# Issuing the remainder-row scores of each eight-unit group two units later, directly ahead of the first scores that use the same K

## The chip, the cores and the metric

The kernel runs on one core of a Trainium2 chip. The metric is the device time of one execution in microseconds (us). Before the change, three runs gave 1204.64, 1207.65 and 1207.88 us, with a median of 1207.65 us.

A core has five engines that matter here, each with an instruction queue of its own that runs in order: TensorE (PE; its weight loads are listed apart as PEld), VectorE (DVE), ScalarE (ACT), GpSimd (POOL) and SyncE (SP), which issues most of the DMA transfers. They are tied together by semaphores alone. Matmul results go to PSUM, which this kernel divides into eight banks with fixed uses; everything else on the chip lies in SBUF.

## The reference, cut to what matters

Two attention blocks, A and B, of the same shape are computed, and their outputs are placed side by side. There are 16 batches, 144 query rows per batch, 16 heads of width 256, 512 keys, and a model width of 448; all data are bf16.

```python
q = (x @ wq).reshape(B, Sq, H, Dh).transpose(0, 2, 1, 3)
scores = einsum("bhqd,bhkd->bhqk", q, k_cache) * (Dh ** -0.5)
p = softmax(scores, axis=-1)
o = einsum("bhqk,bhkd->bhqd", p, v_cache)
out = o.transpose(0, 2, 1, 3).reshape(B, Sq, H * Dh) @ wo
# out = concatenate([out_A, out_B], axis=-1)
```

(`_B_ref` repeats K and V by a factor of 1, so B is A with other data.)

## The kernel before, in words

The work is cut into 512 **units**; a unit is one head of one batch of one block (2 x 16 x 16). The units are numbered in the order block, batch, head. The 144 query rows of a unit are more than one 128-partition tile takes comfortably, so they are split into 112 rows (`QA`), handled unit by unit, and 32 remainder rows (`QB`), handled together: the remainder rows of four units fill one 128-partition tile. The code calls four units G and eight units SG (or n); the 64 groups of eight units share one K tile each, which one transposing DMA loads (`t_load_k`, L368). `kt_sb` has room for three such tiles.

The steps of a unit U and the lines where the profile shows them:

- Q (`t_q`, L398): eight matmuls of the projection into the bank `qp_ps`; a scaled copy to `qt_sb` on DVE (L411) or ACT (L415). `qt_sb` holds 12 units.
- SA (`t_sa`, L516): two matmuls, scores of the 112 rows, into one of two banks `sa_ps`, by the parity of U.
- the row maximum on DVE (`t_max`, L528), the exponential with row sum on ACT (`t_exp`, L539), the reciprocal on DVE (L549), the normalisation on POOL (`t_norm`, L557).
- TA (`t_ta`, L570): four transposes of the 112 rows into the other `sa_ps` bank, and a copy to `pt_sb` on DVE (L580).
- PV (`t_pv`, L603): eight matmuls with V into `ot_ps`, and a copy into `ring` on ACT (L618, L620).
- OP (`t_op_piece`, L641): the output projection of finished 128-row chunks, a few matmuls at a time; the result goes out through ACT (L659) and a store issued from POOL (L671).

The remainder rows of a group n of eight units have their own chain:

- SB (`t_sb`, L440): 16 matmuls of 32 columns, four side by side in the array, which write both `sb_ps` banks, one for each four units. It reads the K tile of group n and the remainder rows in `qt_sb` of all eight units.
- for each of the two fours (G = 2n and 2n + 1): the maximum on DVE (`t_max_b`, L453), the exponential on ACT (`t_exp_b`, L463), the reciprocal on DVE (L473), the normalisation on POOL (`t_norm_b`, L481), the transposes TB on PE (`t_tb`, L493), which write the same `sb_ps` bank, and a copy to `pt_sb` on DVE (`t_evac_ptb`, L502).

The order of the instructions is written out by a loop over **slots** i, from -8 up to the end, with one unit in each stage of a software pipeline per slot. In slot i, PE gets Q of unit i + 15, then SB if a group's slot is i, then SA of unit i + 5, TA of unit i + 2, TB if one is due, PV of unit i, and then OP pieces if any are ready. DVE gets, in that order, the reciprocals of the remainder rows, the scaled copy of Q (in slots that are 2, 4, 6 or 7 modulo 8; in the others ACT has it), the maximum, the reciprocal, the copy after TA, the copy after TB and the maximum of the remainder rows. `_Sched` records this order and adds the semaphore waits that the data and the banks need. Three constants name the lags:

```python
LQ, LS, LT = 15, 5, 2
LSB = 7
```

`LS` is the lag of SA. SB of group n stood in slot 8n - `LSB`; the first two groups have slots of their own (-5 and 3). The rest of the chain hangs on that slot:

```python
s0 = sb_slot[n] + 2 * h          # h = 0, 1; G = 2n + h
at(mxb_at, s0, G); at(exb_at, s0 + 1, G); at(nmb_at, s0 + 2, G)
at(tb_at, max(s0 + 3, 8 * n - 4 + 4 * h), G)
```

OP pieces are ready two slots after the last head of a batch, that is from slots that are 1 modulo 16, and are paced by a credit of 2.25 pieces per slot. In the first 128 slots they run out in the 11th slot, so slots that are 11 to 15 and 0 modulo 16 have none; later there are mostly one or a few such slots per batch.

DMA loads are planned with a slot of release and a deadline (`plan`), sorted by deadline, and all issued from SP, which works them off in order and waits on the semaphores of the buffers that they overwrite. The deadline of a K tile is 8n - `LSB`. x tiles (L294, L295) come every 64 units, the weights of block B (L272, L274) around the middle.

Of the kernel before, what the change touches and what calls it, by code (L numbers as in the profile page):

```python
# [122 lines left out]
def bass_concat_heads__mha_block_cached__gqa_block_cached__near_ridge_kernel(  # L123
# [37 lines left out]
    LQ, LS, LT = 15, 5, 2  # L161
    LSB = 7
# [10 lines left out]
    NSG = NT // 8  # L173
# [4 lines left out]
    with contextlib.ExitStack() as es:  # L178
# [503 lines left out]
        def plan(lo, deadline, lead, fn, *args):  # L682
            dma_plan.append((deadline, len(dma_plan), lo, lead, fn, args))

        sb_slot = [8 * n - LSB for n in range(NSG)]
        sb_slot[0:2] = [-LS, 3]
        q_slot = [u - LQ for u in range(NT)]
        q_slot[0:24] = [-7] * 4 + [-6] * 4 + [-5, -5, -4, -4, -1, -1, 0, 0] + [3, 4, 4, 5, 6, 6, 7, 8]
# [233 lines left out]
```

## Time and profile before

| | |
|---|---|
| three runs, median | 1207.65 us (1204.64 to 1207.88) |
| the profiled execution | 1205.52 us, span 1203.8 us |
| PE busy | 1183.8 us, 98% of the span |
| PEld, DVE, ACT, POOL busy | 75%, 64%, 63%, 56% |
| granted TensorE clock | 1.000 |
| chain that ended last | PE 88%, DMA 6%, DVE 3%, SP queue 3% |
| SA matmuls, mean of one | 385 ns, 1024 of them |
| SB matmuls, mean of one | 382 ns, 1024 of them, four at a time |

In rows of the timeline the first number is the start in us from the start of the span, the second the time in us, then engine, line, operation, destination <- sources, shape and count; in square brackets stands idle time of the engine ahead of the row and what ended it. Matmul starts are recorded while their ends are modelled, so distances between starts are the safer reading on PE.

### The profile page before, as it was taken

Reading aid. Unit: us, or ns where it says so; the run is one execution under the profiler, and the core shown is the slowest. Engines: PE = TensorE matmul, PEld = TensorE weight load, DVE = VectorE, ACT = ScalarE, POOL = GpSimd, SP = SyncE. Lnnn points to the kernel's source line nnn. Section 1 sums busy time; section 2 is a strip of 40 time slices with the busy share of each in tenths; the row PEclk is TensorE's granted clock in tenths of the full one; section 3 lists DMA queues with packets and bytes.
Section 4 is the critical chain, followed back from the end, with each engine's and each line's share of the span. In section 5 each row is a group of like instructions: output and inputs, shape, how many; then the busy total and the mean of one; then the engine's idle time right before and its main releaser. Section 6 shows DMA issues by size and latency. Waiting matters only on the chain.

```text
span 1203.8 us, 34217 instructions
## 1 busy us (share of the span) xinstructions
PE 1183.8 (98%) x14116; PEld 901.8 (75%) x14116; DVE 776.3 (64%) x2190; ACT 762.2 (63%) x2222; POOL 678.4 (56%) x680
## 2 busy tenths in 40 slices
PE   7899999999999999999999999999999999999998
PEld 5677777777777777777777777777777777777776
DVE  4666676666666666666566666666666666666664
ACT  4666666666666666666666666666666666666654
POOL 0565565565565565565555655655655655655554
PEclk9999999999999999999999999999999999999999
DMA  9999999999999999899999999999999999999971
GB/s 304 287 270 280 241 250 244 229 234 241 265 226 227 246 259 246 225 240 234 284 299 265 276 264 272 246 233 238 241 256 230 245 228 261 242 227 244 240 187 48
DMA packets 611130, 294.09 MB, mean 244 GB/s; under 512 B 529696, under 2 KB 538720, under 8 KB 610976
## 3 DMA queue, kind: packets, MB, share of 16 engines
q1 hardware_dynamic: 609344, 288.01, 100.6%
q0 software_dynamic: 1632, 3.90, 1.4%
q8 instruction: 112, 1.84, 0.6%
q14 instruction: 42, 0.34, 0.1%
HBM read 153.61 MB, written 4.13 MB: 131 GB/s over the span
## 4 chain that ended last, share of the span: by engine, by line
PE 88%; DMA 6%; DVE 3%; SPq 3%; ACT 0%; issue 0%; POOL 0%; DVEq 0%
PE ot_ps L603 19%; PE sa_ps L516 18%; PE qp_ps L398 18%; PE op_ps L641 17%; PE sa_ps L570 8%; PE sb_ps L440 5%; DMA kt_sb<-in_B_k_cache_dram 3%; DMA kt_sb<-in_A_k_cache_dram 2%; PE sb_ps L493 2%; DVE stat L528 1%; SPq L294 1%; DMA wq_sb<-in_A_wq_dram 1%; SPq L295 1%; PE qp_ps L641 0%; DVE pt_sb L580 0%; SPq L272 0%
## 5 line engine op out<-in xcount | busy, mean ns | idle before, releaser
L557 POOL TENSOR_TENSOR pa_sb<-pa_sb,stat 112x512 bf16<-112x512 bf16 x512 | 532.6, 1040 | 515.2 <-DVE stat L549 488.5
L539 ACT ACTIVATE pa_sb<-sa_ps,stat 112x512 bf16<-112x512 f32 x512 | 352.0, 688 | 407.3 <-DVE stat L528 406.4
L528 DVE TENSOR_REDUCE stat<-sa_ps 112x1 f32<-112x512 f32 x512 | 353.7, 691 | 321.8 <-PE sa_ps L516 318.6
L398 PEld LDWEIGHTS qp_ps<-xt_sb,wq_sb 128*128 128x128 bf16 x4032 | 283.3, 98 | 80.0 <-DMA wq_sb<-in_A_wq_dram 2.6
L603 PE MATMUL ot_ps<-pt_sb,v_sb 128*128 128x144 bf16 x4096 | 340.4, 226 | 0.0
L398 PE MATMUL qp_ps<-xt_sb,wq_sb 128*128 128x144 bf16 x4032 | 334.5, 226 | 5.6 <-DMA wq_sb<-in_A_wq_dram 3.0
L516 PE MATMUL sa_ps<-kt_sb,qt_sb 128*112 128x512 bf16 x1024 | 310.8, 385 | 0.6 <-DVE pt_sb L580 0.2
L641 PE MATMUL op_ps<-wo_sb,ring 128*128 128x448 bf16 x1120 | 278.8, 352 | 0.0
L603 PEld LDWEIGHTS ot_ps<-pt_sb,v_sb 128*128 128x128 bf16 x4096 | 268.5, 97 | 0.4
L570 PEld LDWEIGHTS sa_ps<-ident,pa_sb 112*128 112x128 bf16 x2048 | 145.4, 97 | 111.0 <-ACT pa_sb L539 23.7
L618 ACT ACTIVATE ring<-ot_ps 128x288 bf16<-128x288 f32 (+8 forms) x512 | 190.3, 372 | 4.4 <-PE ot_ps L603 4.4
L580 DVE COPY pt_sb<-sa_ps 128x448 bf16<-128x448 bf16 x512 | 190.3, 372 | 2.4 <-PE sa_ps L570 2.4
L570 PE MATMUL sa_ps<-ident,pa_sb 112*128 112x112 bf16 x2048 | 185.4, 212 | 0.2
L411 DVE TENSOR_SCALAR qt_sb<-qp_ps 128x288 bf16<-128x288 f32 x250 | 114.1, 457 | 79.4 <-PE qp_ps L398 78.5
L481 POOL TENSOR_TENSOR pb_sb<-pb_sb,stat 128x512 bf16<-128x512 bf16 x128 | 133.1, 1040 | 0.1
L516 PEld LDWEIGHTS sa_ps<-kt_sb,qt_sb 128*112 128x112 bf16 x1024 | 97.0, 129 | 38.7 <-issue 27.2
L641 PEld LDWEIGHTS op_ps<-wo_sb,ring 128*128 128x128 bf16 x1120 | 95.1, 98 | 27.6 <-ACT ring L618 0.2
L415 ACT ACTIVATE qt_sb<-qp_ps 128x288 bf16<-128x288 f32 x254 | 105.2, 414 | 15.5 <-PE qp_ps L398 13.3
L539 ACT ACTIVATION_READ_ACCUMULATOR pa_sb<-sa_ps,stat 112x1 f32 x512 | 99.0, 193 | 0.0
L463 ACT ACTIVATE pb_sb<-sb_ps,stat 128x512 bf16<-128x512 f32 x128 | 88.5, 692 | 0.0
L453 DVE TENSOR_REDUCE stat<-sb_ps 128x1 f32<-128x512 f32 x128 | 86.9, 679 | 0.0
L549 DVE RECIPROCAL stat<-stat 112x1 f32<-112x1 f32 x512 | 78.3, 153 | 0.7 <-ACT pa_sb L539 0.7
(49 smaller groups left out, 420.4 us busy)
## 6 DMA issues: line engine op xcount, KB each, us to landing
v_sb<-in_A_v_cache_dram SPq DMA_DIRECT2D x64, 1024.0 KB, 6.0
v_sb<-in_B_v_cache_dram SPq DMA_DIRECT2D x64, 1024.0 KB, 6.0
out_dram<-ost_sb POOLq DMA_DIRECT2D x34, 112.0 KB, 5.4
wo_sb<-in_A_wo_dram SPq DMA_DIRECT2D x8, 448.0 KB, 6.8
wo_sb<-in_B_wo_dram SPq DMA_DIRECT2D x8, 448.0 KB, 6.1
wq_sb<-in_A_wq_dram SPq DMA_DIRECT2D x4, 768.0 KB, 12.1
wq_sb<-in_B_wq_dram SPq DMA_DIRECT2D x4, 768.0 KB, 7.4
kt_sb<-in_A_k_cache_dram SPq DMA_DIRECT2D x2, 1024.0 KB, 11.0
```

The costliest lines, as they stand in the source:

```text
L398: ins = t.matmul(acc[:, dc * SQ:(dc + 1) * SQ], lhsT=wq_sb[:, kc, c0:c0 + 128], rhs=xt_sb[:, xsl, kc, xo:xo + SQ], start=(kc == 0 and dc = ...
L411: return v.tensor_scalar(qt_sb[:, sl, :, :], src, 1.0 / 16.0, None, op0=ALU.mult)
L481: return g.tensor_tensor(pb_sb[:, psl, :], pb_sb[:, psl, :], stat[:, RINVB + sl:RINVB + sl + 1].to_broadcast([128, SK]), op=ALU.mult)
L516: ins = t.matmul(sa_ps[bank][0:QA, :].rearrange("q (k r) -> q k r", k=KR), lhsT=qt_sb[:, U % NQT, dc, 0:QA], rhs=kt_of(U, dc), start=(dc = ...
L528: return v.tensor_reduce(stat[0:QA, NEG + sl:NEG + sl + 1], sa_ps[bank][0:QA, :], axis=AX.X, op=ALU.max, negate=True)
L539: return a.activation(pa_sb[0:QA, psl, :], sa_ps[bank][0:QA, :], AF.Exp, bias=stat[0:QA, NEG + sl:NEG + sl + 1], scale=1.0, accum_out=stat ...
L557: return g.tensor_tensor(pa_sb[0:QA, psl, :], pa_sb[0:QA, psl, :], stat[0:QA, RINV + sl:RINV + sl + 1].to_broadcast([QA, SK]), op=ALU.mult)
L570: ins = t.transpose(pta_ps[bank][:, c * 128:c * 128 + QA], src[:, c, :], ident[0:QA, 0:QA])
L580: return v.tensor_copy(pt_sb[:, sl, :, 0:QA], pta_ps[bank][:, 0:512].rearrange("p (c q) -> p c q", c=4)[:, :, 0:QA])
L603: ins = t.matmul(ot_ps[ob][:, dc * SQ:(dc + 1) * SQ], lhsT=v_sb[:, vsl, j, c * DH + dc * 128:c * DH + (dc + 1) * 128], rhs=pt_sb[:, sl, c, ...
L618: ins = a.activation(ring[:, 2 * h:2 * h + 2, c0:c0 + n1], src[:, :, 0:n1], AF.Copy)
L641: ins = t.matmul(acc[0:m, 0:D], lhsT=ring[:, c, col0:col0 + m], rhs=wo_sb[:, c, :], start=(c == first), stop=(c == last))
```

## The change

SB of group n moves from slot 8n - 7 to slot 8n - 5, the slot in which SA of unit 8n stands; within the slot SB is ahead of SA. Groups 0 and 1 keep their slots, so 62 of the 64 groups move.

```diff
-        sb_slot = [8 * n - LSB for n in range(NSG)]
+        sb_slot = [8 * n - LS for n in range(NSG)]
         sb_slot[0:2] = [-LS, 3]
```

With SB move, by the same two slots, the maximum, exponential, reciprocal and normalisation of both fours. TB of the first four and the copy after it move from slot 8n - 4 to 8n - 2. TB of the second four stays in slot 8n, as the later of the two terms of `max` is now equal to the earlier. Nothing is added or removed, and `LSB` remains in the deadline of the K loads, so SP's list of DMAs is the same, in the same order.

## The prediction

> **What bounds the kernel now.** I read the page first, then the list of waits, then the timeline of PE around each SB. The page says that PE has almost no idle time to give back. The list of waits says what PE and its weight loads still wait for at SB (L440); columns after the colon are us in total, times, longest.
>
> ```profile
> PE 1183.8 (98%) x14116; PEld 901.8 (75%) x14116; DVE 776.3 (64%) x2190; ACT 762.2 (63%) x2222; POOL 678.4 (56%) x680
> ```
>
> ```profile
> PEld sb_ps L440 <- DVE pt_sb L502: 5.0, 16, 0.9
> ...
> PE sb_ps L440 <- DMA kt_sb<-in_B_k_cache_dram: 3.5, 3, 1.7
> ...
> PE sb_ps L440 <- DMA kt_sb<-in_A_k_cache_dram: 1.8, 2, 1.1
> ```
>
> SB is thus the one place in the steady part where PE waits: five times for a K tile, and 16 times (weight loads only) for the copy after the last TB, which frees the bank. What a wait costs I read from starts on PE, as the distance from the Q ahead of SB to SB. The first pair below waits for nothing (0.60 us), the other five for K.
>
> ```profile
> 127.76 0.66 PE L398 MATMUL qp_ps<-xt_sb,wq_sb 128*128 128x144 bf16 x8
> 128.36 1.05 PE L440 MATMUL sb_ps<-kt_sb,qt_sb 128*32 128x512 bf16 x16
> ...
> 288.40 0.66 PE L398 MATMUL qp_ps<-xt_sb,wq_sb 128*128 128x144 bf16 x8
> 289.81 1.05 PE L440 MATMUL sb_ps<-kt_sb,qt_sb 128*32 128x512 bf16 x16 [0.74 <-DMA kt_sb<-in_A_k_cache_dram]
> ...
> 579.38 0.66 PE L398 MATMUL qp_ps<-xt_sb,wq_sb 128*128 128x144 bf16 x8
> 581.15 1.05 PE L440 MATMUL sb_ps<-kt_sb,qt_sb 128*32 128x512 bf16 x16 [1.10 <-DMA kt_sb<-in_A_k_cache_dram]
> ...
> 599.33 0.66 PE L398 MATMUL qp_ps<-xt_sb,wq_sb 128*128 128x144 bf16 x8
> 601.70 1.05 PE L440 MATMUL sb_ps<-kt_sb,qt_sb 128*32 128x512 bf16 x16 [1.70 <-DMA kt_sb<-in_B_k_cache_dram]
> ...
> 618.05 0.66 PE L398 MATMUL qp_ps<-xt_sb,wq_sb 128*128 128x144 bf16 x8
> 619.39 1.05 PE L440 MATMUL sb_ps<-kt_sb,qt_sb 128*32 128x512 bf16 x16 [0.67 <-DMA kt_sb<-in_B_k_cache_dram]
> ...
> 728.96 0.66 PE L398 MATMUL qp_ps<-xt_sb,wq_sb 128*128 128x144 bf16 x8
> 730.81 1.05 PE L440 MATMUL sb_ps<-kt_sb,qt_sb 128*32 128x512 bf16 x16 [1.18 <-DMA kt_sb<-in_B_k_cache_dram]
> ```
>
> The distances are 1.41, 1.77, 2.37, 1.34 and 1.85 us; less 0.60 each they are 0.81, 1.17, 1.77, 0.74 and 1.25, together 5.7 us. Two of the loads as the chain of waits has them:
>
> ```profile
> 277.09 12.59 DMA kt_sb<-in_A_k_cache_dram
> ...
> 601.33 17.92 DMA kt_sb<-in_B_k_cache_dram
> ```
>
> **The change part by part: the K waits.** SB is the first reader of a K tile; SA of unit 8n reads it two slots later. The change lets SB wait where SA needs the tile anyway, and SP's list and its deadlines stay. A load's landing doesn't move, its first reader does. How much later that is, Q starts two slots after three of the stalls show:
>
> ```profile
> 586.83 0.66 PE L398 MATMUL qp_ps<-xt_sb,wq_sb 128*128 128x144 bf16 x8
> ...
> 606.62 0.66 PE L398 MATMUL qp_ps<-xt_sb,wq_sb 128*128 128x144 bf16 x8
> ...
> 625.82 0.66 PE L398 MATMUL qp_ps<-xt_sb,wq_sb 128*128 128x144 bf16 x8
> ```
>
> From 579.38 to 586.83 are 7.45 us; without the stall (1.17) and without SB itself (1.05) 5.2 us. In the same way 606.62 - 599.33 gives 4.5 and 625.82 - 618.05 gives 6.0. These three loads follow one another, so stalls that vanish add up against the next: the second would be late by 1.77 + 1.17 = 2.9 against 4.5 us, the third by 0.74 + 2.9 = 3.7 against 6.0. The two single ones, 0.81 and 1.25, stand against at least two shortest slots of 1.78 us each (below). No K wait is left; the nearest has 1.6 us to spare. Bounds: -5.7 if all go, 0 if all come back behind slower transfers; I take -5.7, as all five have cover. Behind SB nothing new waits: SA of unit 8n is next on PE and needs the same tile.
>
> By the Trainium skill, "DMA: Bandwidth & Descriptors", Latency and other measured facts, a transposing DMA reaches 261 GB/s; a K tile of 2.1 MB would then take an estimated 8.0 us, land at 285.1, and there would be no K wait to remove, a sum of about 1205 us. The row of 12.59 us is 167 GB/s, so I go by the row.
>
> **The copy that frees the bank.** SB in slot 8n - 7 stands one slot behind TB of the second four. In slots without OP pieces that is too near:
>
> ```profile
> 144.17 0.66 PE L398 MATMUL qp_ps<-xt_sb,wq_sb 128*128 128x144 bf16 x8
> 144.88 1.05 PE L440 MATMUL sb_ps<-kt_sb,qt_sb 128*32 128x512 bf16 x16
> ```
>
> ```profile
> 144.41 0.41 DVE L502 COPY pt_sb<-sb_ps 128x512 bf16<-128x512 bf16 x1
> ```
>
> Q to SB is 0.71 here, 0.11 more than without a wait; 16 times that is 1.8 us, the lower bound of this term. Three slots behind TB the wait goes. What is late next is a loop through DVE, which alone sets slots without OP: SA, maximum (L528), copy after TA (L580), next SA.
>
> ```profile
> 133.78 0.59 PE L516 MATMUL sa_ps<-kt_sb,qt_sb 128*112 128x512 bf16 x2
> ...
> 139.21 0.64 PE L516 MATMUL sa_ps<-kt_sb,qt_sb 128*112 128x512 bf16 x2
> ...
> 140.99 0.64 PE L516 MATMUL sa_ps<-kt_sb,qt_sb 128*112 128x512 bf16 x2
> ...
> 145.86 0.64 PE L516 MATMUL sa_ps<-kt_sb,qt_sb 128*112 128x512 bf16 x2
> ```
>
> ```profile
> 135.09 0.37 DVE L580 COPY pt_sb<-sa_ps 128x448 bf16<-128x448 bf16 x1
> ...
> 135.97 0.45 DVE L411 TENSOR_SCALAR qt_sb<-qp_ps 128x288 bf16<-128x288 f32 x1
> 136.34 0.68 DVE L528 TENSOR_REDUCE stat<-sa_ps 112x1 f32<-112x512 f32 x1
> ...
> 139.89 0.69 DVE L528 TENSOR_REDUCE stat<-sa_ps 112x1 f32<-112x512 f32 x1
> ...
> 140.56 0.37 DVE L580 COPY pt_sb<-sa_ps 128x448 bf16<-128x448 bf16 x1
> ```
>
> One turn is 140.99 - 139.21 = 1.78 us: SA to maximum 0.68, to copy 0.67, to the next SA 0.43. From copy to next maximum the loop thus needs 1.11 us; where the remainder maximum and a scaled Q stand between them, DVE needs 136.34 - 135.09 = 1.25, and the turn is 1.92. Such a pair falls ahead of slots 2 and 4 modulo 8 now, and of 4 and 6 afterwards. Seven times in the first 128 slots, six slots without OP follow each other (11 to 15 and 0 modulo 16). Now they run from SA at 133.78 to SA at 145.86, 12.08 us; less SB (1.05) that is 11.03, with one such pair and one bank wait inside. Afterwards SB of the group stands at the head of the stretch, the next one beyond it; I add 1.78 + 1.92 + 1.78 + 1.92 + 1.78 + 1.78 = 10.96. So the stretches give and take about the same. Upper bound: ACT, which has the remainder exponential in slots 4 and 6, lets TA wait 0.15 longer in both: 7 x 0.30 = +2.1. Between -1.8 and +2.1 I take 0.
>
> **The chains that move.** Maximum, exponential, reciprocal and normalisation keep their distance from SB, so the first four's TB, also moved, sees what it sees now. The second four's TB doesn't move and loses two slots of distance. On PE's, DVE's, ACT's and POOL's queues each moved step passes two slots of other work, on SP's none. In the tightest stretch (normalisations, then the two TBs):
>
> ```profile
> 133.86 1.04 POOL L481 TENSOR_TENSOR pb_sb<-pb_sb,stat 128x512 bf16<-128x512 bf16 x1
> ...
> 138.18 1.03 POOL L481 TENSOR_TENSOR pb_sb<-pb_sb,stat 128x512 bf16<-128x512 bf16 x1
> ```
>
> ```profile
> 136.19 0.39 PE L493 MATMUL sb_ps<-ident,pb_sb 128*128 128x128 bf16 x4
> ...
> 143.44 0.39 PE L493 MATMUL sb_ps<-ident,pb_sb 128*128 128x128 bf16 x4
> ```
>
> The first four has 136.19 - 134.90 = 1.3 us to spare, the second 143.44 - 139.21 = 4.2, which becomes 4.2 - 2 x 1.78 = 0.7. With that cover I cost it at 0; without it, each us late costs up to 62 us over 62 groups. `qt_sb` is released two slots later, two ahead of the next writer: 0.
>
> **The end.** The last SB stands where Q has run out, and waits:
>
> ```profile
> 1165.04 0.66 PE L603 MATMUL ot_ps<-pt_sb,v_sb 128*128 128x144 bf16 x8
> 1166.30 1.05 PE L440 MATMUL sb_ps<-kt_sb,qt_sb 128*32 128x512 bf16 x16 [0.59 <-issue]
> ```
>
> PV to SB is 1.26 us, of which 0.59 is listed as idle: a gain of at most 0.6. Two slots later it stands among OP pieces, but the slot it leaves runs on the loop of 1.78; I take -0.3.
>
> **Sum.** 1205.5 (the profiled execution) - 5.7 + 0 + 0 - 0.3 = 1199.5 us. The median shown, 1207.65, is 2.1 above that execution, the lowest run 0.9 below. K waits are the part that can differ between executions, and they go, so I expect the runs after to lie near the sum rather than 2 us above.
>
> **Rivals.** First, no change: the stalls go where the tile goes. PE comes sooner to each point, loads are issued sooner only where they wait for PE, and a transfer that is slowed by its neighbours (17.92 against 12.59 us) could still be late. For it: loads follow each other without a gap around 600 us. Against: it needs 1.6 us more lateness at the nearest of them. All stalls back: 1205.5 - 0.3, about 1205.
>
> Second, slower: the second four's TB takes over the wait, because POOL's normalisation comes late. From 0.15 us per group (5.7 + 3.6 over 62) it is a loss. With the mean of the bank waits now, 5.0 / 16 = 0.31, it costs 62 x 0.31 = 19: about 1219 us. For it: 0.7 us to spare in the stretches. Against: slots with OP are longer, and POOL is at 56%. The Trainium skill ("SBUF — State Buffer", SBUF: two separate sides) names a mechanism: VectorE in a two-port mode and GpSimd lock a shared port pair for a whole instruction, and the loser waits; moved next to other copies, a normalisation could be held. The row below speaks against such holds so far, with 128 instructions within 15 ns.
>
> ```profile
> L481 POOL TENSOR_TENSOR pb_sb<-pb_sb,stat x128: 1029/1041/1044, 28.9 to 1180.0; 128x512 bf16<-128x512 bf16 x128
> ```
>
> Third, the loop through DVE and ACT loses the +2.1 and 1.8 isn't gained elsewhere: 1199.5 + 2.1 = 1201.6, still faster; it lies in the forecast's own range.
>
> **How the numbers follow.** About 0.3% (3.6 us) is what a measurement of this kernel can tell from no change. The forecast with the third rival has 0.77, its own range 1197 (all bank waits gone too) to 1203; no change 0.13, slower 0.10. The range reaches from 1197 to 1206, so that it holds the first rival and leaves out the second.
>
> **What would show it.** In the profile after, no wait of SB for K or for L502 stands in the list of waits; Q to SB is 0.60 everywhere; the stretches are as long as now; TB (L493) waits at most a few tenths for POOL. It is wrong if K waits reappear at SB, or if L493 waits for L481 in most groups.

## The result, and the profile after

The changed kernel takes 1198.21 us (median of six runs, 1196.96 to 1202.98) against 1206.99 us of the kernel before, run beside it (1204.64 to 1208.68): a ratio of 0.992, with a 95% interval of 0.9901 to 0.9938. The profiled execution took 1198.11 us with a span of 1196.4 us, 7.4 us less than the profiled execution before. The forecast was 1199.5 us, in a range of 1197 to 1206. Of the runs behind the experiments below, one of SB in slot 8n - 6 took 4293.19 us, and its ratio leaves that run out.

The page of the changed kernel: the busy time, and the chain that ended last by engine.

```profile
PE 1181.5 (99%) x14116; PEld 901.0 (75%) x14116; DVE 773.6 (65%) x2190; ACT 758.7 (63%) x2222; POOL 677.0 (57%) x680
...
PE 94%; DVE 3%; SPq 1%; DMA 1%; ACT 0%; issue 0%; DVEq 0%
```

DMA had 6% of the chain before and has 1% now; the SP queue went from 3% to 1%. In the list of what PE waited for in the changed kernel (us in total, times, longest), no SB waits for a K tile any more, and what is left of DMA waits is at the start (L349 is part of the start, too):

```profile
PE qp_ps L398 <- DMA wq_sb<-in_A_wq_dram: 3.3, 4, 1.3
...
PE ot_ps L349 <- DMA kt_sb<-in_A_k_cache_dram: 0.9, 2, 0.6
...
PE sb_ps L440 <- ACT kt_sb L359: 0.7, 1, 0.7
...
PE sb_ps L493 <- POOL pb_sb L481: 0.3, 1, 0.3
```

PE's timeline at the place where SB waited longest before (2.37 us behind Q), group 32, now two slots further on:

```profile
601.44 0.66 PE L398 MATMUL qp_ps<-xt_sb,wq_sb 128*128 128x144 bf16 x8
602.04 1.05 PE L440 MATMUL sb_ps<-kt_sb,qt_sb 128*32 128x512 bf16 x16
```

Q to SB is 0.60 us, and so it is, within about 0.01, for all groups from 2 to 62. Where the time went is best seen by laying the PV starts of the two traces over each other. The table gives the start after less the start before, at some units, and what changed since the row above (worked out from the starts in both traces):

| unit | shift, us | since the row above | what stands there |
|---|---|---|---|
| 8 | +0.10 | | the start |
| 16 | -0.17 | -0.27 | group 2 |
| 112 | -0.05 | +0.12 | six stretches without OP pieces |
| 120 | -0.87 | -0.82 | K wait of group 15 gone |
| 240 | -1.11 | -0.24 | |
| 248 | -2.29 | -1.18 | K wait of group 31 gone |
| 256 | -4.02 | -1.73 | K wait of group 32 gone |
| 264 | -4.76 | -0.74 | K wait of group 33 gone |
| 304 | -5.15 | -0.39 | |
| 312 | -6.55 | -1.40 | K wait of group 39 gone |
| 488 | -6.93 | -0.38 | |
| 511 | -7.42 | -0.49 | the end, last SB |

The five steps at the K waits make 5.87 us of the 7.42, the rest 1.55. (At group 39 the step is 1.40 where the wait itself cost 1.25, so these steps hold a little of the rest too.)

### The profile page after: what moved, and what is told of

The parts are those of the page before. It is cut to its first block, busy times and chain, and to the rows that moved or that the text cites. A ratio compares the mean times of both kernels' runs of the same rounds, so it can differ in the third digit from the quotient of the medians.

```text
span 1196.4 us, 34155 instructions
## 1 busy us (share of the span) xinstructions
PE 1181.5 (99%) x14116; PEld 901.0 (75%) x14116; DVE 773.6 (65%) x2190; ACT 758.7 (63%) x2222; POOL 677.0 (57%) x680
## 4 chain that ended last, share of the span: by engine, by line
PE 94%; DVE 3%; SPq 1%; DMA 1%; ACT 0%; issue 0%; DVEq 0%
PE ot_ps L603 20%; PE qp_ps L398 20%; PE sa_ps L516 19%; PE op_ps L641 18%; PE sa_ps L570 8%; PE sb_ps L440 5%; PE sb_ps L493 2%; DVE stat L528 1%; DMA wq_sb<-in_A_wq_dram 1%; DVE pt_sb L580 1%; DVE stat L453 0%; PE qp_ps L641 0%; SPq L272 0%; SPq L274 0%; DVE qt_sb L411 0%; SPq L379 0%
## 5 line engine op out<-in xcount | busy, mean ns | idle before, releaser
L481 POOL TENSOR_TENSOR pb_sb<-pb_sb,stat 128x512 bf16<-128x512 bf16 x128 | 133.1, 1040 | 0.1
```

Source lines behind the costliest of these rows:

```text
L481: return g.tensor_tensor(pb_sb[:, psl, :], pb_sb[:, psl, :], stat[:, RINVB + sl:RINVB + sl + 1].to_broadcast([128, SK]), op=ALU.mult)
```

## The experiments

Two theories were put against each other. The first: the gain is the K waits, because SB, the first reader of a K tile, asks for it later. The second: the gain is the distance between TB of one group and SB of the next, or where the remainder chain falls among the other work, in all groups alike. In the diffs, `sb_slot` is the slot of SB; each stands against the kernel before unless it says otherwise.

**Five groups alone.**

```diff
-        sb_slot = [8 * n - LSB for n in range(NSG)]
+        sb_slot = [8 * n - (LS if n in (15, 31, 32, 33, 39) else LSB) for n in range(NSG)]
```

> SB is moved to slot 8n - 5 for groups 15, 31, 32, 33 and 39 alone, the five that waited for K in the profile before; the other groups keep slot 8n - 7. If the gain is the K stalls, this keeps most of it: 1207.0 - 5.9 = about 1201 us, some 2 us above the changed kernel, and no SB of these five waits for K. If the gain comes from the distance between TB and SB in all groups, it stays near 1206.

Measured: 1203.95 us, ratio 0.9974 (0.9962 to 0.9987). None of the five waits for K, and their places give 0.81, 1.18, 0.74 and 1.40 us at units 120, 248, 264 and 312, as in the table. But most of the gain is missing: by the medians 2.7 us are gained, where about 6 were expected. The profile (the slowest of the twelve runs) shows two new waits in the timeline of PE: group 37, which did not wait before and was not moved, waits for its K tile, and behind group 32 a Q waits for block B's weights.

```profile
695.53 1.05 PE L440 MATMUL sb_ps<-kt_sb,qt_sb 128*32 128x512 bf16 x16 [1.85 <-DMA kt_sb<-in_B_k_cache_dram]
```

```profile
611.69 0.66 PE L398 MATMUL qp_ps<-xt_sb,wq_sb 128*128 128x144 bf16 x8 [2.82 <-DMA wq_sb<-in_B_wq_dram]
```

So late K tiles aren't always the same five: that of group 37 landed at 695.40 us, 3.0 us later than in the kernel before, though PE was only 0.2 us later there. The expectation took the waits of one execution for a list. Another 1.83 us of this profile were lost ahead of unit 8, where the granted clock fell to 0.50 between 24 and 26 us; this is no effect of the edit, which changes nothing there.

**All groups but these five.**

```diff
+        sb_slot = [8 * n - (LSB if n in (15, 31, 32, 33, 39) else LS) for n in range(NSG)]
```

> The complement: all groups move but 15, 31, 32, 33 and 39. If the gain is the K stalls, about 1.5 to 2.5 us remain (about 1205 us) and the five SB wait for K again, by 0.7 to 2.4 us each. If it is the distance between TB and SB, about 1199 to 1200 us.

Measured: 1203.89 us, 0.9974 (0.9957 to 0.9992). Two of the five (32 and 39) wait, longer than before, as the list of waits has it; five were expected to wait:

```profile
PE sb_ps L440 <- DMA kt_sb<-in_B_k_cache_dram: 4.9, 2, 2.6
```

Each half is worth about 2.7 us by the medians, and the whole change 8.8: the halves don't add up, which the first theory in its simple form had not said. A wait that is taken away at one group brings PE sooner to the next unmoved one, and the tile there is sooner by less: at group 32, PE reached the Q ahead of SB 2.67 us sooner than in the kernel before, and the tile landed 1.75 us sooner. The three other unmoved groups (15, 31 and 33) waited for no tile; theirs landed 3.3, 2.7 and 2.4 us sooner than before. Where a wait shows thus differs from trace to trace.

**SB unmoved, x loads earlier.**

```diff
-                plan(lo, dl, 40, t_load_x, XG)
+                plan(lo, dl - 4, 40, t_load_x, XG)
```

> SB stays in slot 8n - 7 and the deadlines of the x loads are four slots earlier, so that an x load stands ahead of a V load that waits for PE, and no longer between that V load and the K load. If the stalls come from what stands ahead of the K load on SP, the waits at groups 15 and 39 go (-0.8 and -1.3) and those at 31 to 33 shrink or go (up to -3.7): 1201 to 1205 us, with nothing on PE moved. If K tiles are late because the DMA engines are full, no wait goes and the time stays at 1207.

Measured: 1201.67 us, 0.9957 (0.9941 to 0.9973). This is the cleanest evidence for the first theory: no instruction of PE, DVE, ACT or POOL changed places, and 5 us went by the medians. Of the 3.83 us between the two profiles, 3.82 went at the same five groups. On the SP queue the x load now stands ahead of the V load that waits for PE, and the K tile of group 15 is issued at 270.01 us where it was 277.09:

```profile
262.96 3.12 SPq L294 DMA_TRANSPOSE xt_sb<-in_A_x_dram  x1
266.12 1.86 SPq L295 DMA_TRANSPOSE xt_sb<-in_A_x_dram  x1
269.59 0.37 SPq L379 DMA_DIRECT2D v_sb<-in_A_v_cache_dram  x1
270.01 10.70 SPq L368 DMA_TRANSPOSE kt_sb<-in_A_k_cache_dram  x1
```

What PE still waits at SB, by the list of waits, is less than a third of before (groups 32, 33 and 39; that of 39 was expected to go):

```profile
PE sb_ps L440 <- DMA kt_sb<-in_B_k_cache_dram: 1.5, 3, 0.6
```

**Half of the way.**

```diff
+        sb_slot = [8 * n - 6 for n in range(NSG)]
```

> SB in slot 8n - 6, half of the way. The bank wait is gone (two slots behind TB), and a K tile has one slot of 1.8 to 2.4 us more. Stalls of 0.8, 1.2, 0.7 and 1.3 us are covered, the one of 1.8 (2.9 once the one ahead of it has gone) is left with up to 0.9: about 1199 to 1200 us, and one or two K waits in the list. If the time were set by where the remainder chain falls among the Q copies on DVE, it would differ from both kernels in either direction by more than 2 us.

Measured: 1207.92 us, 1.0002 (0.9989 to 1.0014). A clear miss: the K waits shrank as expected (one is left, 1.5 us at group 32), and the gain was given back elsewhere, by about 0.5 us in each stretch without OP pieces. PE's list of waits shows where (this kernel; the changed kernel has 2.2 us, 3 times, in the first of these rows and 1.7 us, once, in the second):

```profile
PEld qp_ps L398 <- ACT qt_sb L415: 13.9, 29, 1.8
PE qp_ps L398 <- ACT qt_sb L415: 8.4, 26, 1.7
```

and the timelines of ACT and PE of the same kernel in one such stretch:

```profile
133.74 0.70 ACT L463 ACTIVATE pb_sb<-sb_ps,stat 128x512 bf16<-128x512 f32 x1
134.31 0.22 ACT L463 ACTIVATION_READ_ACCUMULATOR pb_sb<-sb_ps,stat 128x1 f32 x1
134.40 0.43 ACT L415 ACTIVATE qt_sb<-qp_ps 128x288 bf16<-128x288 f32 x1
```

```profile
134.88 0.68 PE L398 MATMUL qp_ps<-xt_sb,wq_sb 128*128 128x144 bf16 x8 [0.21 <-ACT qt_sb L415]
```

The scaled copy of Q has one PSUM bank, and the next Q waits until it is copied out. With SB in slot 8n - 6 the remainder exponentials fall into slots 3 and 5 modulo 8, in which the Q copy is ACT's, and stand ahead of it. This is a third theory: a slot for SB is good or bad by whether the exponentials behind it fall into slots where DVE has the Q copy.

**Half of the way, with the Q copies' pattern moved along.** Against the kernel of the experiment above:

```diff
-            if (U - LQ) % 8 in (2, 4, 6, 7):
+            if (U - LQ) % 8 in (3, 5, 7, 0):
```

> SB in slot 8n - 6 as in the run that gained nothing (1208), with the scaled copies of Q on DVE in slots 3, 5, 7 and 0 modulo 8 instead of 2, 4, 6 and 7, so that ACT never has a Q copy in the slot of a remainder exponential. If that run lost its gain because Q waited for a Q copy behind that exponential on ACT (+0.5 us per batch with a stretch), this one takes 1198 to 1201 us, at most with a K wait at group 32. If it lost it to something else in slot 8n - 6, it stays at 1206 to 1208.

Measured: 1199.86 us, 0.994 (0.9925 to 0.9955), by the ratios 7.5 us faster than with the old pattern. The list of waits has the Q wait back at its old size, and a K wait of 2.6 us at group 32, which was expected (the other of the two, 0.2 us, is at group 33):

```profile
PEld qp_ps L398 <- ACT qt_sb L415: 2.2, 3, 1.9
...
PE sb_ps L440 <- DMA kt_sb<-in_B_k_cache_dram: 2.7, 2, 2.6
```

The third theory holds for this slot. The new pattern wasn't run with SB in slot 8n - 7 or 8n - 5, so whether it is better by itself isn't shown. Per stretch this kernel even gains where the changed one is even: its shift goes from -0.18 at unit 16 to -0.85 at unit 112.

**One slot beyond.**

```diff
+        sb_slot = [8 * n - 4 for n in range(NSG)]
```

> SB in slot 8n - 4, one slot behind the first SA that reads the same K. SA then is the first reader of K, where SB is in the changed kernel, so K gets no more room, and both TBs move one slot. If the K stalls and the bank wait were all, the time is that of the changed kernel within 1 us (1197 to 1199). If moving SB later went on paying, it would be another 3 us or more faster.

Measured: 1203.89 us, 0.9967 (0.9955 to 0.9979); expected were 1197 to 1199. No SB waits for K. PE waits for the Q copy again, 5.9 us at 11 places where the changed kernel has 1.7 us at one. The shift against the kernel before rises by about 0.3 us per stretch, and between units 248 and 256 only 0.13 us are gained instead of 1.73, as a Q waits for block B's weights:

```profile
609.93 0.66 PE L398 MATMUL qp_ps<-xt_sb,wq_sb 128*128 128x144 bf16 x8 [1.56 <-DMA wq_sb<-in_B_wq_dram]
```

**One slot beyond, with the pattern moved along.** The same edit of the pattern as above.

> The same for SB in slot 8n - 4 (1204 without it): 1197 to 1200 us by the theory of the Q copy behind the exponential, 1203 to 1205 if it is the slot itself.

Measured: 1202.32 us, 0.9959 (0.9945 to 0.9972). The stretches no longer lose (shift -0.31 at unit 16, -0.18 at unit 112, where the old pattern went from -1.10 to +0.76), so the pattern is confirmed here too, but the median is 2 us above the expected 1197 to 1200. In its profile 2.72 us are lost between units 248 and 256 against the kernel before, which itself lost 1.73 there. Block B's weights are waited for again:

```profile
PE qp_ps L398 <- DMA wq_sb<-in_B_wq_dram: 2.3, 1, 2.3
```

The wait is not all of it. Behind it the same eight matmuls of PV take 1.17 us, and those of the next unit 0.67 again:

```profile
609.92 0.66 PE L398 MATMUL qp_ps<-xt_sb,wq_sb 128*128 128x144 bf16 x8 [2.33 <-DMA wq_sb<-in_B_wq_dram]
...
611.54 1.17 PE L603 MATMUL ot_ps<-pt_sb,v_sb 128*128 128x144 bf16 x8
...
614.33 0.67 PE L603 MATMUL ot_ps<-pt_sb,v_sb 128*128 128x144 bf16 x8
```

The view by windows of 1 us (window, PE busy and count, granted clock, DMA) has the reason, a granted clock that goes down behind the wait:

```profile
609.00:610.00 1.00, 0.08 (x2) 1.00 1.05 375
610.00:611.00 1.00, 1.00 (x10) 0.76 1.07 363
611.00:612.00 1.00, 1.00 (x9) 0.50 1.33 128
612.00:613.00 1.00, 1.00 (x11) 0.50 1.24 280
613.00:614.00 1.00, 1.00 (x8) 0.53 1.28 290
614.00:615.00 1.00, 1.00 (x17) 1.00 1.27 290
```

What is missing to 1.00 in these windows adds up to 1.7 us. That is an estimate of what the lower clock cost on top of the wait.

**The bank wait alone.** SB stays in slot 8n - 7, and TB of the second four comes two slots earlier, so that the bank is free sooner; `pt_sb` needs 12 buffers for it, and the output buffer goes from 3 to 2 for the space.

```diff
-    NQT, NPA, NPB, NPT, NST, NSTB, NOST = 12, 5, 2, 8, 4, 2, 3
+    NQT, NPA, NPB, NPT, NST, NSTB, NOST = 12, 5, 2, 12, 4, 2, 2
...
-                at(tb_at, max(s0 + 3, 8 * n - 4 + 4 * h), G)
+                at(tb_at, s0 + 3, G)
```

> As the kernel before, SB in slot 8n - 7, but TB of the second four two slots earlier (8n - 2), with the same 12 and 2 buffers. Only the wait for the bank goes; K is wanted as early as before. If the gain is the K stalls, they stay (0.7 to 2.4 us at groups 15, 31, 32, 33, 39) and at most 1.8 us are gained: 1205 to 1207. If the bank wait was what mattered, 1199 to 1200.

Measured: 1205.39 us, 0.9978 (0.9964 to 0.9993). In the list of waits the bank has gone from 16 times and 5.0 us to once, and K waits stand at four of the five groups (31, 32, 33 and 39):

```profile
PE sb_ps L440 <- DMA kt_sb<-in_B_k_cache_dram: 5.1, 3, 3.5
...
PEld sb_ps L440 <- DVE pt_sb L502: 0.2, 1, 0.2
```

The K wait of group 32, 3.47 us here, is again followed by a granted clock of 0.50 (603 to 606 us). The bank is worth 1.9 us by the medians, 0.26 per batch by the traces (shift 1.05 at unit 16, -0.51 at unit 112, six batches). The second theory thus has a share, but a small one.

**The cover of the second four's TB taken away.** Against the changed kernel, TB of the second four stands one slot earlier, with the same buffers as above:

```diff
-                at(tb_at, max(s0 + 3, 8 * n - 4 + 4 * h), G)
+                at(tb_at, s0 + 3 - h, G)
```

> As the changed kernel, but TB of the second four is one slot earlier (8n - 1 instead of 8n), two slots behind its maximum; pt_sb gets 12 buffers instead of 8 and the output buffer 2 instead of 3, to make it possible. It takes away the cover that was put at 0.7 us in the tightest stretch. If that cover was real and thin, TB now waits for POOL by about 0.5 to 1 us in each group and the kernel loses some 25 to 60 us (1223 to 1258). If the chain had far more room than computed, nothing changes (1198).

Measured: 1248.82 us, 1.034 (1.0313 to 1.0367), 50.6 us more than the changed kernel, 0.82 us per moved group. TB waits for POOL's normalisation in each of the 64 groups:

```profile
PEld sb_ps L493 <- POOL pb_sb L481: 50.3, 64, 1.2
PE sb_ps L493 <- POOL pb_sb L481: 40.2, 64, 1.0
```

One slot less, and the rival that ends slower is there. The price of it was real, and the cover in the changed kernel is less than a slot wide.

**The changed kernel with x loads earlier.** The edit of the x loads above, made to the changed kernel.

> The changed kernel with the x loads' deadlines four slots earlier. If the changed kernel waits for no K tile in any run, earlier loads bring nothing: 1198 within 1 us. If some of its runs still lose time to late tiles (one run took 1203), the spread or the median falls.

Measured: 1197.29 us, 0.9908 (0.9885 to 0.9931), four runs from 1196.91 to 1197.91. This is the fastest median of all, but its interval overlaps that of the changed kernel, so it isn't shown to be faster. Once SB asks late, loads that come sooner bring next to nothing, as the first theory says.

**Fourteen groups.**

```diff
+        late = (7, 15, 23, 31, 32, 33, 34, 35, 36, 37, 38, 39, 47, 55)
+        sb_slot = [8 * n - (LS if n in late else LSB) for n in range(NSG)]
```

> SB moves for the 14 groups whose K load has x or block B weight loads just ahead of it or among its neighbours on SP (7, 15, 23, 31 to 39, 47, 55), the others stay. Five groups gave 1204, with a K wait at group 37 in the profile. If late K tiles at these 14, not always the same ones, are what the change removes, this gives 1199 to 1202, and no SB waits for K by more than a few tenths; if the rest of the gain sits in the 48 groups left behind, it stays at 1203 to 1204.

Measured: 1203.03 us, 0.9956 (0.9941 to 0.9972), five runs from 1199.1 to 1204.07. The median is a miss for the first theory: it lies in the 1203 to 1204 that were expected if the rest of the gain sits in the other groups. The trace says something else. The profiled run (1200.65) has no K wait at SB, and the one DMA wait behind the start that the changed kernel doesn't have is again that for block B's weights. From unit 16 to the end this kernel gains 3.0 us less than the changed one, and 2.50 of that between units 248 and 256:

```profile
608.59 0.66 PE L398 MATMUL qp_ps<-xt_sb,wq_sb 128*128 128x144 bf16 x8 [2.46 <-DMA wq_sb<-in_B_wq_dram]
```

The three slower runs have a granted clock of 0.998 or 0.999, the two faster ones 1.000. Of the three there is no profile, so what they lost stays open, and with it which theory the median speaks for.

**x loads and block B's query weights earlier.** Against the changed kernel:

```diff
-                plan(lo, dl, 40, t_load_x, XG)
+                plan(lo, dl - 4, 40, t_load_x, XG)
...
-                dl = pr * NU + 4 * hg - LQ if pr > 0 else (-59, -57, -55, -52)[hg]
+                dl = pr * NU + 4 * hg - LQ - 4 if pr > 0 else (-59, -57, -55, -52)[hg]
```

> The changed kernel with the x loads and block B's query weights (L272, L274) both four slots earlier in the list. Two runs showed Q waiting for those weights (2.8 and 1.6 us) once the K wait ahead of it had gone. With both early there is no DMA wait after the start: 1196 to 1198 us, with a narrow spread; if earlier weights delay K tiles instead, K waits come back and it is 1199 or more.

Measured: 1198.16 us, 0.9923 (0.9907 to 0.994), four runs from 1197.34 to 1198.78. No Q waits for block B's weights, and a K wait comes back at group 32, as the weights now stand ahead of its tile. One wait is paid for with the other; no gain over the changed kernel.

```profile
PE sb_ps L440 <- DMA kt_sb<-in_B_k_cache_dram: 0.6, 1, 0.6
```

## Why the prediction was right

**K waits.** Taken as -5.7 us; the table gives -5.87. Half of the step held: the first reader moved back, and no SB waits. That SP's order makes the tiles late is shown by the run in which only the x loads moved. The other half, "a load's landing doesn't move", is not what the traces show. Times in us, from the two traces:

| group | issued, before / after | landed, before / after | SB starts, after |
|---|---|---|---|
| 15 | 277.09 / 274.97 | 289.67 / 288.00 | 294.85 |
| 31 | 567.30 / 565.90 | 581.01 / 578.48 | 584.02 |
| 32 | 583.15 / 580.38 | 601.56 / 600.40 | 602.04 |
| 33 | 601.33 / 600.18 | 619.25 / 619.56 | 620.54 |
| 39 | 718.17 / 714.00 | 730.67 / 726.17 | 728.81 |

```profile
718.17 9.66 SPq L368 DMA_TRANSPOSE kt_sb<-in_B_k_cache_dram  x1
```

```profile
714.00 7.91 SPq L368 DMA_TRANSPOSE kt_sb<-in_B_k_cache_dram  x1
```

All five loads were issued sooner and four landed sooner, and what stands ahead of them on SP waits for PE, in the changed kernel the V loads above all:

```profile
SPq L379 <- PE op_ps L641: 223.4, 52, 12.6
```

At group 15, where PE was only 0.05 us ahead, the 1.7 us can't come from that; they differ so between executions. It mattered at two groups. PE comes to group 39 about 5.1 us sooner, all gains before it together, and the working had held only that group's own 1.25 us against the two slots. Had the tile landed at 730.67 as before, SB would have waited about 2 us. At group 32 the spare was reckoned as 1.6 us. By the old landing it would have been under 0.5, as the gains before group 31 were left out there; since the tile landed 1.16 us sooner it was 1.64 after all. Two errors thus cancelled, and that the wait went at all five groups is in part luck. The tightest tile was that of group 33, landed 0.98 us ahead of SB.

The step also left out what is late next. "Behind SB nothing new waits" is true of the profiled execution of the changed kernel, but block B's weights are close behind: four other kernels, with the same list of DMAs, waited 1.6 to 2.8 us for them. One of the six runs of the changed kernel took 1202.98, at a granted clock of 0.997 where the other five have 1.000; whether such a wait stands behind it isn't shown.

**The bank.** Taken as 0 between -1.8 and +2.1. From unit 16 to 112 the shift moves by only +0.12: eight units with a stretch lose 0.13, and the eight with the next SB, whose bank wait is gone, gain 0.12. So give and take are as reckoned there. The first two turns of a stretch in the changed kernel, and its last, by the starts of SA:

```profile
133.47 0.64 PE L516 MATMUL sa_ps<-kt_sb,qt_sb 128*112 128x512 bf16 x2
...
135.25 0.64 PE L516 MATMUL sa_ps<-kt_sb,qt_sb 128*112 128x512 bf16 x2
...
137.16 0.64 PE L516 MATMUL sa_ps<-kt_sb,qt_sb 128*112 128x512 bf16 x2
...
142.64 0.64 PE L516 MATMUL sa_ps<-kt_sb,qt_sb 128*112 128x512 bf16 x2
...
144.54 0.59 PE L516 MATMUL sa_ps<-kt_sb,qt_sb 128*112 128x512 bf16 x2
```

It lasts 11.07 us where 10.96 was added up; the turns of 1.78 and 1.91 are those of the loop through DVE, and the last turn, 1.90, is a third long one where two were reckoned. Part of the wait did move into other steps: the list of weight loads has, in the changed kernel,

```profile
PEld sa_ps L570 <- ACT pa_sb L539: 26.2, 98, 0.6
PEld sa_ps L516 <- DVE pt_sb L580: 3.2, 11, 0.4
```

against 23.7 us at 84 places and 0.9 us at 3 before. SB was thus not "the one place in the steady part" where PE's weight loads wait. Between units 16 and 488, outside the six batches and the five K steps, and at group 2, the table has another -1.28 us (-0.27, -0.24, -0.39 and -0.38), which the working had not looked at. That single slots without OP pieces make it is argued, not shown. The term was mis-sized by about 1.2 us.

**The chains that move.** The second four's cover was put at 0.7 us. The rows of POOL and PE in the stretch give 143.31 - 142.63 = 0.68:

```profile
137.91 1.03 POOL L481 TENSOR_TENSOR pb_sb<-pb_sb,stat 128x512 bf16<-128x512 bf16 x1
141.59 1.04 POOL L481 TENSOR_TENSOR pb_sb<-pb_sb,stat 128x512 bf16<-128x512 bf16 x1
```

```profile
139.62 0.39 PE L493 MATMUL sb_ps<-ident,pb_sb 128*128 128x128 bf16 x4
143.31 0.39 PE L493 MATMUL sb_ps<-ident,pb_sb 128*128 128x128 bf16 x4
```

For the first four the step was wrong: it was to keep its 1.3 us and has 139.62 - 138.94 = 0.68 as well, as its chain now lies wholly in slots without OP pieces. It was enough. No normalisation was held by DVE in its new place: the 128 of L481 still lie between 1029 and 1043 ns, so nothing here shows the port lock of the Trainium skill ("SBUF — State Buffer", SBUF: two separate sides) at work between these instructions.

**The end.** Taken as -0.3; -0.49 in the table.

**The sum and the median.** 1205.5 - 6.0 = 1199.5 was forecast, 1198.11 came in the profiled execution, the difference being the 1.2 us of the bank term and about 0.2 each of the K waits and the end, less the 0.1 of the start. The medians lie further apart than the two profiled executions, 8.8 against 7.4 us, since the kernel before was 1.5 us slower in the median than in its profile. The prediction had expected this, with K waits as the part that varies; that the tiles that are late differ between traces (group 37 late in one, 15, 31 and 33 on time in another) supports it.

The granted clock is a second part that varies, which the working didn't have. Beside the experiments the kernel before ran 61 times: nine runs had a clock of 1.000 and a median of 1206.09 us, fifteen had 0.997 and 1208.13. Of the six runs of the changed kernel five had 1.000. With the clock at 1.000 on both sides the medians are 1206.09 and 1198.16, 7.9 us apart, so the clock is not what makes the gain, but it can stand behind a part of what the medians show beyond the profiles.

**The rivals.** That the stalls come back behind slower transfers did not happen in the changed kernel, but the two halves show some of it: three unmoved groups in all (37 in one, 32 and 39 in the other) wait by 1.9 to 2.6 us. That TB takes over the wait needed one slot more than the change took.

## What to carry to other kernels

Where PE is the bound and work stands in a written-out order, look for the first reader of each late transfer, and ask whether it must be first: moving the reader back to where the data is needed anyway gave more here (8.8 us) than moving a load forward in the list (about 5). Before counting such a wait as gained, name the transfer that is late next, add up all that PE gains before it, ask whether the load itself waits for PE and so comes sooner too, and don't take the waits of one execution for a list. And when a chain is moved by a slot, check it against every alternating assignment of engines: SB in slot 8n - 6 gave nothing where slot 8n - 5 gave 8.8 us, and moving the pattern of the Q copies along brought 7.5 back.

## What was not expected of the hardware

- A late tile follows PE only in part. Where SB of group 32 kept slot 8n - 7, its tile landed at 601.56 us in the kernel before, at 601.35 with the bank freed and at 599.81 with the rest moved, while PE had reached the Q ahead of SB at 599.33, 597.26 and 596.66. What PE had gained before that tile was lost at it mostly in the second case and by a third in the last one (waits of 1.7, 3.5 and 2.6 us of idle PE).
- A long wait of PE can cost more than its length. Four times, in three traces, a granted clock of 0.50 follows idle time of PE, for some 3 us and at an estimated cost of 1.7 us each time (1 less the clock, summed over the windows): behind a wait of 2.33 us for weights, behind one of 3.47 us for K, and near 23 us, in the start, with five groups moved and with the bank freed. Waits of 2.46, 2.6 and 2.8 us in other traces were not followed by it, so the length alone doesn't decide.
- A transposing DMA of 2.1 MB keeps the SP queue for 10.70 us in the row of the run with early x loads (7.9 to 16.5 us in the changed kernel, but for one of 20.4 that waited for PE), and an x load 3.12 + 1.86 us. What stands behind it in the list is issued only then: with early x loads the V and K loads behind them show it in the rows.
